# Causal attention and a gated feed-forward on one core: engine orders searched anew, with the 16-bit product sums kept apart from GpSimd's masks in the plan

## Chip, core and metric

The kernel runs on one core of a Trainium2 chip. The metric is device time in microseconds (us) of one launch; the time before is the median of three runs, 325.62 us. Engines are named as the profile names them: PE (TensorE; PEld its weight loads), DVE (VectorE), ACT (ScalarE), POOL (GpSimd) and SP (SyncE). POOL computes the masks and also issues most of the loads; SP issues stores and transposing transfers.

## What is computed

Inputs are float32. Attention has 8 batches, 8 heads, 576 tokens, 64 features a head, and 16 extra "beacon" keys that every query sees. Its result, 4608 tokens by 512 features, goes through a feed-forward of width 2048.

```python
k_all = np.concatenate([beacon_k, k], axis=2)
v_all = np.concatenate([beacon_v, v], axis=2)
scores = scale * np.matmul(q, k_all.transpose(0, 1, 3, 2))
causal[:, Nb:] = np.triu(np.ones((S, S), dtype=bool), k=1)
scores = np.where(causal, -1000000000.0, scores)
a = np.exp(scores - scores.max(-1, keepdims=True))
a /= a.sum(-1, keepdims=True) + 1e-09
x = np.matmul(a, v_all)                  # then tokens by heads*features
h = x @ w_in                             # 512 -> 2048
g = h * (1.0 / (1.0 + np.exp(-1.702 * h)))
out = g @ w_out                          # 2048 -> 512
```

## The kernel before

**Attention.** Work is cut into 16 sets (a batch and four of its heads; set s belongs to batch s // 2). For a set, PE makes scores in chunks (`e_qk`, L557 and L568, into the score banks `s`), ACT exponentiates a chunk into the fp16 tile `E` (`e_exp`, L580), and POOL sets the masked triangle of each key block to zero in place (`e_mask`, L598). From set 4 on, four DVE sums add the key blocks of `E` into `zs` (`e_zadd`, L616), so that PE's row-sum matmuls are short. A set then has four value tiles on PE (`e_av`, L656): first the row sums (name `av s.2.0`), which DVE transposes, inverts and spreads (`e_z1` L666, `e_z2` L672 and L677), then `av s.0.0`, `av s.0.1`, `av s.1.1`, each multiplied by the inverse on DVE and put into `xT` (`e_norm`, L694).

**Feed-forward.** Tokens go in groups: groups 0 and 1 of 256, groups 2 to 9 of 512. The first layer of a group is either plain (`e_m1`, L718) or, for part of the later groups, a seven-product Strassen form: products `f g.i.1` to `f g.i.7` (`e_part`, L923), with DVE sums of weights (`wsum`) and tokens (`xsum`) before them, ACT copies between them (`seedb`, `seede` L933, `keep7` L939) and DVE sums in PSUM after them (`sum22`, `sum21`, L942). ACT applies the gate (L740, L948). The second layer of groups 2 to 9 is a seven-product Strassen form too: `e_prod` (L836), named `m2.g.p.n0` for product p. DVE makes its inputs with the **product sums** `s g.i.n0` (16 of 128 x 512 fp16 a group, 128 in all, both inputs in SBUF) and its outputs with the joins (`e_join`, L852), which add a product in PSUM to `osb` and so free its PSUM bank. All two-input fp16 sums of DVE, product sums among them, go through `add`, L784.

**Banks.** Four PSUM banks are shared in turn by value tiles, first-layer tiles and products; four more serve the scores or, late, the Strassen tiles. `BANK` says which bank each tile takes. A tile that takes a bank waits for whatever reads the tile before it there.

**Order.** Nothing on the chip schedules. Each unit of work is an operation of a `Plan`, numbered in the order in which the kernel names them; `ORDER` gives for every engine the list of these numbers, found by a search outside the kernel, and `Plan.run` lays the lists out in time by fixed costs. The operations are emitted by planned start, and each engine then runs its own list strictly in turn; dependences become semaphore waits. In `Plan.run` an operation with `port` 1 (certain DVE sums) starts no earlier than the end of the last one with `port` 2 (POOL masks), and the other way round. That rule exists in the plan alone: nothing of it is emitted, and the chip runs two such instructions whenever their lists and semaphores let it.

Numbers used below: 362, 367 and 373 are group 2's joins of products 7, 5 and 4; 348, 349 and 350 its product sums `s2.2.*`; 375 is PE's `m2.2.3.0`; 488 a `wsum`, 490 to 493 group 3's `xsum`, 481 and 485 norms of set 5; 494 is `f3.0.1`; 626 is `qk27`. 1011 is `z2` of set 11 and 938 group 5's join of product 2; 993 and 1016 are `av10.1.1` and `av11.1.1`; 925 to 928, 934, 936, 914 to 920 are product sums of group 5. 1225 is `z2` of set 13, 1095 group 6's join of product 2, 1230, 1179 and 1177 are `av13.1.1`, `av12.1.1` and `av12.0.1`, 1103 is `m2.6.7.2`; 1082 to 1085, 1091 and 1094 are product sums of group 6. 402 and 403 are the transposes of set 4's keys and queries, 404 is `qk16`. 795 is the last mask of set 8, 800 the `zadd` that needs it, 801 `av8.2.0`, 845 a mask of set 9 that needs the exponentials 814 and 843.

Of the kernel before, what the change touches and what calls it, by code (L numbers as in the profile page):

```python
# [18 lines left out]
        126, 136, 162, 165, 231, 129, 168, 171, 236, 147, 150, 152, 131, 245, 238, 174, 177, 241, 192, 195, 262,  # L19
        201, 198, 204, 267, 248, 207, 210, 186, 269, 250, 252, 276, 187, 180, 272, 213, 188, 404, 181, 182, 183,  # L20
        189, 407, 257, 255, 283, 281, 288, 286, 279, 410, 222, 223, 224, 225, 417, 314, 296, 320, 300, 308, 298,
        312, 294, 310, 306, 324, 302, 316, 318, 334, 322, 304, 343, 216, 435, 426, 335, 217, 218, 219, 438, 336,
        344, 345, 337, 358, 353, 467, 359, 346, 354, 355, 356, 363, 364, 597, 429, 477, 360, 361, 433, 600, 431,
        482, 484, 480, 605, 365, 369, 366, 494, 370, 624, 371, 372, 375, 498, 376, 626, 496, 377, 503, 378, 502,
        516, 510, 500, 530, 512, 514, 526, 506, 518, 519, 538, 522, 532, 528, 540, 536, 534, 550, 559, 629, 615,
        551, 552, 560, 553, 569, 561, 570, 780, 574, 575, 571, 562, 572, 783, 576, 579, 577, 580, 638, 786, 618,
        622, 620, 643, 792, 641, 645, 581, 582, 585, 810, 651, 586, 587, 657, 588, 813, 591, 592, 593, 594, 655,
        653, 842, 659, 660, 663, 667, 697, 689, 693, 671, 669, 673, 685, 675, 676, 687, 695, 683, 679, 691, 707,
        801, 852, 968, 708, 716, 717, 718, 719, 709, 710, 804, 971, 859, 806, 857, 808, 855, 976, 742, 726, 727,
        743, 736, 728, 995, 731, 732, 737, 729, 733, 997, 738, 734, 739, 744, 745, 865, 1000, 748, 869, 749,  # L30
        750, 751, 871, 881, 887, 867, 873, 883, 874, 885, 905, 877, 889, 890, 907, 893, 903, 897, 921, 911, 899,
        901, 909, 922, 1009, 986, 1151, 923, 930, 931, 932, 940, 941, 924, 933, 1154, 993, 1016, 1012, 989, 942,
        1157, 945, 943, 1014, 991, 1163, 956, 946, 950, 951, 947, 1181, 948, 957, 1022, 952, 953, 1184, 958,
        959, 962, 1026, 963, 964, 965, 1213, 1031, 1024, 1030, 1062, 1028, 1038, 1064, 1044, 1068, 1034, 1042,
        1040, 1054, 1046, 1047, 1066, 1050, 1056, 1087, 1060, 1058, 1088, 1172, 1223, 1355, 1089, 1078, 1079,
        1080, 1090, 1081, 1102, 1103, 1358, 1230, 1179, 1177, 1228, 1175, 1363, 1104, 1107, 1097, 1098, 1226,
        1382, 1099, 1100, 1108, 1105, 1109, 1384, 1113, 1114, 1110, 1236, 1115, 1387, 1119, 1120, 1238, 1121,
        1116, 1240, 1242, 1252, 1258, 1122, 1245, 1244, 1254, 1268, 1373, 1256, 1248, 1284, 1270, 1260, 1261,
        1272, 1288, 1290, 1264, 1286, 1396, 1276, 1292, 1274, 1277, 1293, 1401, 1380, 1376, 1378, 1403, 1399,
        1280, 1308, 1296, 1317, 1409, 1309, 1425, 1318, 1319, 1411, 1310, 1427, 1311, 1429, 1320, 1327, 1431,  # L40
        1415, 1332, 1433, 1413, 1328, 1434, 1437, 1329, 1330, 1417, 1333, 1441, 1334, 1421, 1335, 1445, 1443,
        1337, 1447, 1457, 1418, 1338, 1339, 1459, 1449, 1463, 1340, 1461, 1453, 1450, 1481, 1465, 1343, 1344,
        1466, 1482, 1483, 1349, 1490, 1345, 1469, 1346, 1491, 1350, 1532, 1351, 1352, 1548, 1492, 1536, 1534,
        1493, 1484, 1505, 1550, 1552, 1506, 1516, 1507, 1517, 1556, 1554, 1500, 1501, 1557, 1502, 1503, 1518,
        1508, 1538, 1560, 1540, 1541, 1564, 1519, 1510, 1511, 1568, 1512, 1570, 1513, 1544, 1573, 1572, 1566,
        1522, 1580, 1523, 1524, 1525, 1584, 1576, 1586, 1582, 1588, 1589, 1604, 1605, 1613, 1606, 1592, 1614,
        1615, 1628, 1629, 1607, 1630, 1616, 1633, 1623, 1631, 1624, 1625, 1626, 1634, 1635, 1636, 1637, 1641,
        1642, 1643, 1647, 1644, 1648, 1651, 1652,
# [3 lines left out]
        237, 239, 175, 178, 242, 193, 196, 263, 199, 202, 205, 268, 208, 211, 270, 273, 405, 214, 190, 184, 408,  # L52
        411, 418, 419, 321, 226, 309, 299, 297, 301, 315, 295, 325, 317, 311, 307, 303, 313, 319, 323, 305, 436,
        220, 439, 468, 342, 469, 598, 601, 607, 606, 495, 625, 499, 627, 497, 511, 501, 531, 517, 515, 507, 509,
        505, 513, 539, 525, 533, 527, 529, 521, 541, 523, 537, 535, 630, 558, 781, 784, 787, 793, 794, 811, 658,
        652, 814, 656, 843, 844, 662, 668, 666, 654, 690, 698, 672, 674, 664, 686, 670, 678, 694, 688, 696, 682,
        684, 680, 692, 969, 715, 972, 977, 978, 996, 998, 866, 1001, 870, 882, 872, 868, 886, 884, 888, 880,
        906, 876, 878, 904, 908, 892, 894, 898, 896, 912, 900, 902, 910, 1152, 929, 1155, 1158, 1165, 1164,
        1182, 1023, 1185, 1027, 1214, 1215, 1025, 1029, 1065, 1039, 1033, 1063, 1045, 1043, 1035, 1055, 1037,
        1069, 1049, 1067, 1053, 1051, 1041, 1061, 1057, 1059, 1356, 1086, 1359, 1364, 1365, 1383, 1385, 1237,  # L60
        1388, 1239, 1241, 1253, 1243, 1259, 1255, 1251, 1269, 1257, 1247, 1249, 1285, 1271, 1263, 1273, 1267,
        1289, 1265, 1287, 1291, 1275, 1295, 1279, 1281, 1297, 1283, 1410, 1426, 1412, 1299, 1428, 1316, 1430,
        1432, 1436, 1414, 1438, 1416, 1442, 1440, 1420, 1422, 1444, 1446, 1458, 1448, 1424, 1460, 1462, 1452,
        1464, 1456, 1454, 1468, 1472, 1470, 1533, 1549, 1535, 1551, 1553, 1489, 1555, 1559, 1537, 1539, 1563,
        1565, 1561, 1543, 1569, 1571, 1545, 1547, 1575, 1581, 1579, 1585, 1567, 1583, 1587, 1577, 1591, 1593,
        1595, 1612, 1656,
# [3 lines left out]
        228, 127, 229, 259, 157, 164, 161, 167, 128, 130, 170, 173, 148, 149, 153, 151, 132, 246, 260, 176, 261,  # L70
        179, 194, 197, 247, 200, 203, 249, 206, 401, 209, 212, 403, 253, 254, 277, 251, 402, 278, 215, 258, 284,
        282, 256, 285, 416, 414, 280, 287, 415, 289, 422, 423, 424, 425, 486, 290, 291, 292, 326, 487, 329, 327,
        427, 331, 339, 333, 330, 338, 328, 428, 332, 293, 473, 340, 341, 474, 351, 357, 475, 476, 349, 347, 478,
        430, 479, 434, 432, 483, 485, 481, 490, 491, 362, 492, 350, 348, 367, 373, 493, 488, 489, 379, 504, 611,
        508, 520, 524, 612, 613, 542, 634, 614, 546, 545, 544, 554, 543, 547, 555, 548, 556, 616, 617, 549, 557,
        635, 563, 564, 567, 636, 637, 573, 578, 639, 640, 619, 565, 623, 621, 642, 644, 646, 647, 648, 583, 649,
        650, 589, 566, 595, 661, 797, 798, 665, 799, 848, 677, 699, 703, 681, 849, 800, 850, 851, 701, 700, 704,
        702, 802, 803, 711, 720, 853, 854, 712, 706, 805, 724, 705, 807, 713, 860, 856, 721, 809, 722, 858, 714,
        730, 861, 862, 863, 735, 740, 746, 723, 1005, 864, 752, 875, 1006, 879, 891, 913, 917, 1007, 895, 982,
        983, 984, 914, 985, 1008, 918, 925, 926, 915, 987, 919, 988, 1010, 1011, 934, 927, 936, 916, 938, 920,  # L80
        994, 935, 928, 990, 1013, 1017, 1018, 944, 1015, 1168, 937, 992, 1169, 949, 1019, 1020, 954, 1021, 960,
        1170, 966, 1219, 1220, 1032, 1036, 1048, 1052, 1073, 1221, 1070, 1171, 1071, 1075, 1077, 1222, 1072,
        1173, 1174, 1076, 1074, 1224, 1225, 1083, 1085, 1094, 1095, 1082, 1231, 1084, 1180, 1091, 1229, 1178,
        1176, 1369, 1370, 1227, 1232, 1093, 1101, 1233, 1371, 1106, 1234, 1235, 1092, 1111, 1392, 1117, 1372,
        1123, 1250, 1246, 1374, 1393, 1394, 1262, 1266, 1395, 1375, 1397, 1398, 1294, 1278, 1402, 1381, 1377,
        1282, 1379, 1400, 1300, 1304, 1301, 1312, 1298, 1302, 1405, 1406, 1407, 1306, 1305, 1313, 1408, 1321,
        1404, 1314, 1325, 1322, 1303, 1307, 1323, 1315, 1435, 1439, 1331, 1419, 1336, 1423, 1451, 1473, 1324,
        1474, 1455, 1341, 1467, 1478, 1475, 1479, 1471, 1487, 1347, 1528, 1529, 1477, 1353, 1476, 1496, 1485,
# [1458 lines left out]
```

## Time and profile before

| | us |
|---|---|
| median of 3 runs (325.38 to 325.70) | 325.62 |
| the profiled execution | 324.99 |
| its span, first to last instruction | 323.3 |
| busy: PE / PEld / DVE / ACT / POOL | 310.8 / 227.6 / 243.4 / 226.9 / 137.6 |
| granted TensorE clock, mean | 0.997 |
| share of 16 DMA engines: queue of POOL's loads / queue of the rest | 68.9% / 23.6% |

A profile row names an engine, a line of the kernel, the tiles written and read and a shape. A busy PE need not be PE at its peak, since matmuls are pipelined; so the waits, in which an engine stood idle for a named semaphore, are read beside the busy time. Rows of the timeline give start and length in us, "x4" merges neighbours of one kind, and brackets hold the idle time before a row and what ended it. Four PE matmuls of 256 columns start 0.44 us apart from the next four.

### The profile page before, as it was taken

Reading aid. Unit: us, or ns where it says so; the run is one execution under the profiler, and the core shown is the slowest. Engines: PE = TensorE matmul, PEld = TensorE weight load, DVE = VectorE, ACT = ScalarE, POOL = GpSimd, SP = SyncE. Lnnn points to the kernel's source line nnn. Section 1 sums busy time; section 2 is a strip of 40 time slices with the busy share of each in tenths; the row PEclk is TensorE's granted clock in tenths of the full one; section 3 lists DMA queues with packets and bytes.
Section 4 is the critical chain, followed back from the end, with each engine's and each line's share of the span. In section 5 each row is a group of like instructions: output and inputs, shape, how many; then the busy total and the mean of one; then the engine's idle time right before and its main releaser. Section 6 shows DMA issues by size and latency. Waiting matters only on the chain.

```text
span 323.3 us, 9042 instructions
## 1 busy us (share of the span) xinstructions
PE 310.8 (96%) x3835; PEld 227.6 (70%) x3835; DVE 243.4 (75%) x481; ACT 226.9 (70%) x297; POOL 137.6 (43%) x188
## 2 busy tenths in 40 slices
PE   6999999999997999999999989999999999999994
PEld 2567765545775667766788567766688888888883
DVE  4759893786989779768977798839977993775682
ACT  1778967567766896699668975798689658546720
POOL 8768658798469802175248105570132000000000
PEclk9999999999999999999999999999999999999998
DMA  6999999999999993559099933998006000020202
GB/s 116 175 203 193 173 197 159 162 118 132 204 110 141 205 153 62 76 141 131 2 92 98 149 100 49 179 134 78 2 3 146 4 32 3 0 99 32 100 33 99
DMA packets 125993, 34.67 MB, mean 107 GB/s; under 512 B 111488, under 2 KB 123904, under 8 KB 125952
## 3 DMA queue, kind: packets, MB, share of 16 engines
q0 software_dynamic: 91872, 18.57, 68.9%
q1 hardware_dynamic: 33872, 15.45, 23.6%
q8 instruction: 30, 0.49, 0.6%
q10 hardware_dynamic: 208, 0.07, 0.1%
q14 instruction: 11, 0.09, 0.1%
HBM read 37.22 MB, written 15.42 MB: 163 GB/s over the span
## 4 chain that ended last, share of the span: by engine, by line
PE 44%; DVE 10%; ACT 5%; issue 1%; DVEq 0%; ACTq 0%
PE u L836 21%; PE u L923 15%; PE u L656 4%; PE s L557 3%; DVE g L784 2%; PE u L718 2%; DVE zs L616 2%; DVE rz L677 2%; ACT g L948 1%; DVE sA L784 1%; ACT g L740 1%; DVE zt L666 1%; DVE u L942 1%; DVE osb L852 1%; ACT u L933 1%
## 5 line engine op out<-in xcount | busy, mean ns | idle before, releaser
L580 ACT ACTIVATE E<-s 128x2048 f16<-128x2048 f32 (+3 forms) x59 | 90.8, 1553 | 36.7 <-PE s L557 23.9
L598 POOL TENSOR_SCALAR_AFFINE_SELECT E<-E 128x512 f16<-128x512 f16 (+3 forms) x78 | 60.2, 850 | 103.7 <-ACT E L580 85.1
L836 PEld LDWEIGHTS <-g 128*128 128x128 f16 x768 | 73.1, 98 | 14.4 <-issue 3.2
L836 PE MATMUL u<-w,g 128*128 128x256 f16 x512 | 67.5, 273 | 1.7 <-DVE osb L852 1.7
L718 PE MATMUL u<-xT,w 128*128 128x512 f16 (+1 forms) x320 | 60.4, 337 | 0.0
L948 ACT ACTIVATE g<-u 128x512 f16<-128x512 f32 x80 | 46.6, 617 | 14.0 <-PE u L923 7.2
L852 DVE SCALAR_TENSOR_TENSOR osb<-u,osb 128x512 f32<-128x512 f32 (+2 forms) x51 | 33.2, 655 | 20.0 <-PE u L836 18.0
L718 PEld LDWEIGHTS <-w 128*128 128x128 f16 x320 | 30.5, 98 | 20.5 <-issue 0.3
L472 POOL DMA_DIRECT2D vb<-in_v_dram x32 | 40.1, 1259 | 0.6 <-issue 0.6
L923 PEld LDWEIGHTS <-SF 128*128 128x128 f16 x320 | 30.9, 98 | 8.0 <-issue 1.4
L836 PE MATMUL u<-tB,g 128*128 128x256 f16 x256 | 34.9, 273 | 0.0
L923 PE MATMUL u<-sig,SF 128*128 128x256 f16 x240 | 34.4, 273 | 0.1
L933 ACT ACTIVATE u<-u 128x512 f32<-128x512 f32 x40 | 23.6, 593 | 10.0 <-PE u L923 8.7
L656 PE MATMUL u<-E,vb 128*32 128x352 f16 (+8 forms) x928 | 28.1, 263 | 2.3 <-DVE osb L852 1.6
L740 ACT ACTIVATE g<-u 128x512 f16<-128x512 f32 x48 | 27.3, 637 | 4.0 <-PE u L718 3.8
L694 DVE TENSOR_TENSOR xT<-u,rz 128x352 f16<-128x352 f32 (+6 forms) x58 | 26.0, 478 | 5.3 <-PE u L656 4.8
L784 DVE TENSOR_TENSOR g<-g 128x512 f16<-128x512 f16 x64 | 28.3, 455 | 0.6
L656 PEld LDWEIGHTS <-vb 128*32 128x32 f16 (+1 forms) x928 | 20.3, 96 | 9.2 <-issue 4.8
L923 PEld LDWEIGHTS <-w 128*128 128x128 f16 x240 | 23.2, 98 | 3.4 <-issue 0.3
L616 DVE TENSOR_TENSOR zs<-zs,E 128x1344 f16<-128x1344 f16 (+2 forms) x36 | 22.1, 619 | 4.5 <-POOL E L598 3.4
L923 PE MATMUL u<-xT,w 128*128 128x256 f16 x160 | 23.7, 273 | 0.0
L486 POOL DMA_DIRECT2D qD<-in_q_dram x10 | 23.1, 2365 | 0.0
(72 smaller groups left out, 431.6 us busy)
## 6 DMA issues: line engine op xcount, KB each, us to landing
out_dram<-osb SPq DMA_DIRECT2D x35, 256.0 KB, 3.3
vb<-in_v_dram POOLq DMA_DIRECT2D x24, 128.0 KB, 7.2
qD<-in_q_dram POOLq DMA_DIRECT2D x10, 288.0 KB, 8.6
kD<-in_k_dram POOLq DMA_DIRECT2D x10, 288.0 KB, 9.8
w<-in_moe_w_in_dram POOLq DMA_DIRECT2D x8, 256.0 KB, 8.5
w<-in_moe_w_out_dram POOLq DMA_DIRECT2D x4, 512.0 KB, 10.9
kn<-in_k_dram POOLq DMA_DIRECT2D x6, 288.0 KB, 6.8
qn<-in_q_dram POOLq DMA_DIRECT2D x6, 288.0 KB, 6.9
```

What stands on the lines that cost most here:

```text
L472: nc.gpsimd.dma_start(out=t[0 : hi - lo, j, h0:h1, :], in_=v[b, h0:h1, lo:hi, :].rearrange("h n d -> n h d"),)
L580: nc.scalar.activation(out=Es[s][:, h0:h1, c0:c1], in_=sall[(i, p)][:, :, o : o + c1 - c0], func=AFT.Exp, scale=0.125,)
L598: nc.gpsimd.affine_select(out=blk, in_=blk, compare_op=ALU.is_ge, fill=0.0, base=off + (Nb if j == 0 else 0), pattern=[[0, Q], [1, w]], ch ...
L616: nc.vector.tensor_tensor(out=t, in0=E[:, :, Z0:S] if i == 1 else t, in1=E[:, :, wcol[i] : wcol[i] + S - a], op=ALU.add,)
L656: nc.tensor.matmul(u[32 * h : 32 * h + 32, a:e], lhs, src[0:kw, h, col : col + e - a], start=first, stop=last, skip_group_check=s >= EARLY ...
L718: nc.tensor.matmul(u[:, o + a - t0 : o + e - t0], w1t[:, kp, nt * P : (nt + 1) * P], xT[:, kp, a % XR : (e - 1) % XR + 1], start=(kp == 0 ...
L740: nc.scalar.activation(out=gts[g][:, n0:n1, 0:w], in_=rings[("m1", g, n0)][:, 0 : n * w].rearrange("p (n w) -> p n w", n=n), func=AFT.Gelu ...
L784: (nc.vector if eng == "DVE" else nc.gpsimd).tensor_tensor(out=out, in0=a, in1=b, op=op)
L836: nc.tensor.matmul(u[:, HM * mt : HM * (mt + 1)], lhs[:, n, mt * P : (mt + 1) * P], rhs[:, n, :], start=(n == 0 and (mt == 0 or apart) and ...
L852: nc.vector.scalar_tensor_tensor(out=osbs[(g, dst)][:, c0:c1], in0=rings[("p", g, p)][:, c0:c1], scalar=scale_of(g), in1=osbs[(g, src)][:, ...
L923: nc.tensor.matmul(u[:, HM * n : HM * (n + 1)], lhs[x][:, (2 * i + n) * P : (2 * i + n + 1) * P], rhs[:, x, :], start=fresh and n == 0 and ...
L948: nc.scalar.activation(out=gts[g][:, n : n + 2, HM * h : HM * (h + 1)], in_=rings[src][:, :].rearrange("p (n w) -> p n w", n=2), func=AFT. ...
```

## The change

`Plan.op` strips digits and dots, no longer digits alone, from the end of an operation's name before it looks it up in `HELD`. Names of product sums (`s2.0.4`) so end as `s`, which is in `HELD`; before, they ended as `s2.0.`, which is not. `zadd`, `xsum`, `wsum`, `t`, DVE's own masks and `bk` had matched already. With that rule `ORDER` and `BANK` were searched anew. The set of operations, their dependences and what each emits are the same (3826 matmuls in both programs); the positions differ: 184 of PE's 578 list entries stand where they stood, 101 of DVE's 437, 135 of ACT's 288 and 40 of POOL's 181, with mean moves of 2.6, 2.9, 1.6 and 7.6 places. The count of PE's changes between its three tilings is 128 in both.

```diff
-        elif eng == "DVE" and name.rstrip("0123456789") in HELD:
+        elif eng == "DVE" and name.rstrip("0123456789.") in HELD:
             o.port = 1
```

Of `ORDER`, the places that the prediction speaks of:

```diff
     "PE": [
-        201, 198, 204, 267, 248, 207, 210, 186, 269, 250, 252, 276, 187, 180, 272, 213, 188, 404, 181, 182, 183,
+        201, 198, 204, 267, 248, 207, 210, 186, 269, 252, 250, 276, 187, 180, 272, 181, 182, 213, 404, 188, 183,
...
-        482, 484, 480, 605, 365, 369, 366, 494, 370, 624, 371, 372, 375, 498, 376, 626, 496, 377, 503, 378, 502,
+        482, 484, 480, 605, 365, 366, 369, 370, 494, 624, 371, 372, 375, 498, 376, 626, 377, 503, 378, 496, 502,
...
-        901, 909, 922, 1009, 986, 1151, 923, 930, 931, 932, 940, 941, 924, 933, 1154, 993, 1016, 1012, 989, 942,
+        909, 921, 986, 1009, 1151, 930, 922, 923, 931, 932, 933, 924, 940, 1154, 941, 1016, 993, 1012, 989,
...
-        1080, 1090, 1081, 1102, 1103, 1358, 1230, 1179, 1177, 1228, 1175, 1363, 1104, 1107, 1097, 1098, 1226,
+        1088, 1089, 1090, 1081, 1102, 1358, 1230, 1179, 1228, 1177, 1175, 1363, 1097, 1098, 1107, 1099, 1226,
     "DVE": [
-        179, 194, 197, 247, 200, 203, 249, 206, 401, 209, 212, 403, 253, 254, 277, 251, 402, 278, 215, 258, 284,
+        176, 179, 247, 197, 194, 200, 206, 249, 203, 414, 209, 212, 253, 254, 277, 251, 402, 278, 403, 215, 256,
...
-        430, 479, 434, 432, 483, 485, 481, 490, 491, 362, 492, 350, 348, 367, 373, 493, 488, 489, 379, 504, 611,
+        478, 479, 434, 432, 483, 488, 481, 485, 362, 490, 367, 349, 491, 492, 493, 373, 350, 489, 611, 379, 612,
...
-        983, 984, 914, 985, 1008, 918, 925, 926, 915, 987, 919, 988, 1010, 1011, 934, 927, 936, 916, 938, 920,
+        984, 917, 985, 1008, 914, 918, 987, 915, 919, 988, 1010, 925, 927, 916, 936, 926, 1011, 938, 1017, 920,
...
-        1173, 1174, 1076, 1074, 1224, 1225, 1083, 1085, 1094, 1095, 1082, 1231, 1084, 1180, 1091, 1229, 1178,
+        1173, 1072, 1076, 1174, 1224, 1225, 1084, 1095, 1091, 1075, 1231, 1180, 1083, 1092, 1229, 1176, 1178,
     "POOL": [
-        826, 1125, 633, 631, 632, 785, 812, 788, 796, 822, 815, 846, 845, 782, 789, 828, 838, 766, 768, 1197,
+        632, 818, 633, 768, 772, 1125, 785, 1133, 1195, 788, 1191, 812, 845, 832, 776, 789, 815, 782, 1193, 770,
...
-        795, 1131, 973, 1133, 834, 847, 980, 1187, 970, 999, 830, 832, 1003, 1143, 1002, 836, 1004, 1135, 981,
+        796, 846, 1129, 836, 795, 970, 830, 999, 1141, 834, 980, 1003, 981, 1189, 1004, 979, 838, 828, 847, 973,
```

164 rows, old and new, of tables (BANK, ORDER) are left out of this document.

## The prediction

> **What bounds the kernel now.** Read first were the page's busy times and slices, then the view of who waited for whom.
>
> ```profile
> PE 310.8 (96%) x3835; PEld 227.6 (70%) x3835; DVE 243.4 (75%) x481; ACT 226.9 (70%) x297; POOL 137.6 (43%) x188
> ...
> PE   6999999999997999999999989999999999999994
> ...
> DVE  4759893786989779768977798839977993775682
> ```
>
> PE sets the time: it is busy in nearly every slice, and both programs have the same matmuls and as many changes of tiling. An order can win only what PE waits. Those waits (waiter, waited for: total us, times, longest) are:
>
> ```profile
> PE u L836 <- DVE osb L852: 1.7, 1, 1.7
> PE u L656 <- DVE osb L852: 1.6, 2, 1.0
> ...
> PE u L923 <- DVE u L942: 0.7, 2, 0.4
> PE u L656 <- DVE xT L694: 0.6, 2, 0.3
> ```
>
> That is 4.6 us in seven places, all for DVE: the ceiling of the gain, since other engines' waits matter only where PE ends up in one of its own.
>
> **What a clash costs.** The view of line 784 (times in ns, min/median/max) and the view by lines (busy us, mean ns) of the product sums:
>
> ```profile
> L784 DVE TENSOR_TENSOR g<-g x64: 381/418/1276, 79.2 to 312.4; 128x512 f16<-128x512 f16 x64
> ...
> L784 DVE TENSOR_TENSOR g<-sA,g x32: 382/420/1339, 79.7 to 311.4; 128x512 f16<-128x512 f16 x32
> ```
> ```profile
> L784 DVE TENSOR_TENSOR g<-g 128x512 f16<-128x512 f16 x64 | 28.3, 455 | 0.6
> ...
> L784 DVE TENSOR_TENSOR g<-sA,g 128x512 f16<-128x512 f16 x32 | 15.4, 488 | 0.8
> ```
>
> A product sum takes 0.42, and up to 1.34. The excess of the means over the medians is 64 x 37 + 32 x 68 ns = 4.5 us. This is DVE time; it counts only where a join or a norm queued behind it lets PE go. So I go to PE's waits one by one and ask what each becomes in the new lists.
>
> **Stall A, at 99 us.** Timelines (start, length) of DVE, POOL, PE and ACT:
>
> ```profile
> 93.23 1.09 DVE L694 TENSOR_TENSOR xT<-u,rz 128x352 f16<-128x352 f32 x2 [0.46 <-PE u L656]
> 94.63 1.06 DVE L694 TENSOR_TENSOR xT<-u,rz 128x352 f16<-128x352 f32 x2 [0.30 <-PE u L656]
> ...
> 96.08 0.96 DVE L784 TENSOR_TENSOR sig<-xT,sig 128x512 f16<-128x512 f16 x1
> 96.97 0.68 DVE L852 SCALAR_TENSOR_TENSOR osb<-u,osb 128x512 f32<-128x512 f32 x1
> 97.57 0.80 DVE L784 TENSOR_TENSOR sig<-xT,sig 128x512 f16<-128x512 f16 x1
> 98.29 2.01 DVE L784 TENSOR_TENSOR g<-g 128x512 f16<-128x512 f16 x2
> 100.22 1.48 DVE L852 SCALAR_TENSOR_TENSOR osb<-u,osb 128x512 f32<-128x512 f32 x2
> ```
> ```profile
> 97.72 2.13 POOL L472 DMA_DIRECT2D vb<-in_v_dram  x1
> 98.62 3.26 POOL L598 TENSOR_SCALAR_AFFINE_SELECT E<-E 128x512 f16<-128x512 f16 x3
> ```
> ```profile
> 98.17 1.05 PE L836 MATMUL u<-tB,g 128*128 128x256 f16 x8
> 100.95 0.60 PE L836 MATMUL u<-w,g 128*128 128x256 f16 x4 [1.74 <-DVE osb L852]
> ```
> ```profile
> 98.28 1.88 ACT L580 ACTIVATE E<-s 128x2048 f16<-128x2048 f32 x1
> ```
>
> Product sums 350 and 348 stand before join 367 and, against three masks, take 2.01 instead of twice 0.42; the join starts at 100.22 and `m2.2.3.0` waits 1.74. In the new lists both stand elsewhere. After the second norm (ends 94.3) come `wsum` 488 (as much data as three to four product sums, 1.3), two norms and join 362 (0.6 each), `xsum` 490 (0.4), then 367. The 0.30 in which DVE waited is filled; the norms end near 96.6, 362 near 97.2, 490 near 97.6, and 367 at 98.25, before PE asks at 99.0. The wait goes: -1.74. But the norms end some 0.9 later than they did (94.63 + 1.06 = 95.7), and `f3.0.1`, which needs them, stands 0.44 later in PE's list. So its copy on ACT, and the exponential queued behind it (98.28, ends 100.16), end 0.45 later, at 100.6, and `qk27` waits for its score bank where PE comes at 100.3. I take 0.45 back: **-1.3**. Bounds: -1.74; and -0.5, if 490 and 488 suffer as the rows of 0.96 and 0.80 did (the second while POOL only issued a load).
>
> [...]
>
> **Stall B, at 193 us.** DVE, then PE:
>
> ```profile
> 190.60 0.38 DVE L784 TENSOR_TENSOR g<-g 128x512 f16<-128x512 f16 x1
> 190.91 0.80 DVE L784 TENSOR_TENSOR g<-sA,g 128x512 f16<-128x512 f16 x1
> ...
> 192.49 0.68 DVE L852 SCALAR_TENSOR_TENSOR osb<-u,osb 128x512 f32<-128x512 f32 x1
> ```
> ```profile
> 191.51 0.75 PE L656 MATMUL u<-E,vb 128*32 128x352 f16 x20
> 193.22 1.33 PE L656 MATMUL u<-E,vb 128*32 128x352 f16 x52 [0.96 <-DVE osb L852]
> ```
>
> Four product sums, one of 0.80, stand between inverse 1011, which ends at 190.6, and join 938, which frees the bank of `av11.1.1`. After, three of them stand ahead of 1011 and 938 follows it directly: 1011 ends some 1.0 later, at 191.6 (three sums, 0.34 from one start to the next), 938 at 192.3. `BANK` gives `av11.1.1`, now first, a bank that product 1 held: it needs only 1011 and waits 0.2 beyond 191.5. `av10.1.1` takes 938's bank and waits 0.15. 0.96 becomes 0.35: **-0.6** (0 to -0.96).
>
> **Stall C, at 228 us.** DVE, then PE:
>
> ```profile
> 225.49 1.16 DVE L784 TENSOR_TENSOR g<-sA,g 128x512 f16<-128x512 f16 x2
> ...
> 227.03 0.68 DVE L852 SCALAR_TENSOR_TENSOR osb<-u,osb 128x512 f32<-128x512 f32 x1
> ```
> ```profile
> 227.76 2.19 PE L656 MATMUL u<-E,vb 128*32 128x352 f16 x76 [0.65 <-DVE osb L852]
> ```
>
> Three product sums between 225.49 and join 1095 become one, and `av12.1.1` takes product 1's bank instead of the join's. The 0.65 goes; but `m2.6.7.2` (0.44), which filled PE while `qk50` had its exponential pending, now comes later, and some 0.25 of it is lost: **-0.4** (-0.65 to +0.2). The smaller of the two waits on L942 (0.24, `f8.1.3` at 266 us) ends too, since five other pieces of PE, not three, now stand between `f8.1.5`, which its sum needs, and `f8.1.3`: **-0.2** (0 to -0.24). The other waits keep their neighbours: 0.
>
> **New waits.** Query transpose 403 moves behind key transpose 402 and inverse 278. DVE, then PE:
>
> ```profile
> 47.50 1.26 DVE L523 STREAM_TRANSPOSE kT<-kn 128x576 f32<-128x576 f32 x1
> ...
> 48.82 0.48 DVE L677 STREAM_TRANSPOSE rz<-rc 128x288 f32<-128x288 f32 x1
> ```
> ```profile
> 49.51 0.63 PE L568 MATMUL s<-qT,kT 32*128 32x512 f16 x8
> 50.07 3.63 PE L764 MATMUL u<-w,g 128*128 128x512 f16 x16
> ```
>
> 278 ends at 49.3 now, and 0 to 1.1 earlier with 403 gone from ahead of it; 403 (1.26, as 402) then ends between 49.5 and 50.6. `qk16`, which needs it, comes one PE piece later (four such take 3.63), at 50.4: **+0.2** (0 to 0.5). Near 85 us two product sums move ahead of set 5's `zadd`, in a stretch where the slices show DVE 8 or 9 tenths busy, and `av5.2.0` waits for that `zadd`: **+0.1** (0 to 0.7, both sums). A walk finds old waits more surely than new ones; for those not found I add **+0.3**, an estimate: one more wait of the size of the smaller ones above (0 to 3, the sizes of A, B and `qk16` together).
>
> POOL's loads move most (sets 8 to 15). I cost that at nothing: what hides it are the tens of us between those loads and their sets' first use. The price where that cover is thin is rival 1.
>
> Sum: -1.3 - 0.6 - 0.4 - 0.2 + 0.2 + 0.1 + 0.3 = **-1.9**. The profiled execution's own 324.99 (span 323.3 and 1.7 around it) becomes 323.1. It was 0.63 below the median, so the median goes from 325.62 to **323.7**.
>
> **Rivals.**
>
> 1. *Masks late behind loads (slower).* All of set 8's late masks now stand behind mask 845, which waits for the later of two exponentials, and six masks and six issues, 845 among them, come before mask 795, which `zadd` 800 and then `av8.2.0` need. The exponentials, PE, and POOL's busy time (count) per stretch, fifth pair of numbers, and one issue's length in the crowded stretch from 60 to 140 us:
>
> ```profile
> 139.99 1.94 ACT L580 ACTIVATE E<-s 128x1024 f16<-128x1024 f32 x2
> ```
> ```profile
> 152.47 0.38 PE L656 MATMUL u<-zs,ones 128*32 128x288 f16 x8
> ```
> ```profile
> 60.00:80.00 20.00, 20.00 (x144) 9.65 (x143) 13.56 (x20) 13.63 (x22) 19.54 (x21) 1.00 1.86 127
> ...
> 140.00:160.00 20.00, 19.30 (x224) 12.90 (x227) 17.23 (x32) 18.33 (x26) 8.97 (x12) 1.00 0.73 111
> ```
> ```profile
> L472 POOL DMA_DIRECT2D vb<-in_v_dram x10 | 19.9, 2000 | 0.0
> ```
>
> 845 starts at 141.0. At 8.97 / 12 = 0.75 an instruction, 795 as the thirteenth ends at 150.8, in time for 152.5. At 19.54 / 21 = 0.93 it ends at 153.1, and from there each 0.1 costs PE 1.3. At 1.15, between that and the 2.0 of a single issue, it ends at 156.0 and PE stands 3.5: 325.6 + 3.5 - 1.9 = 327.2. Against it: POOL has 0.75 in that very stretch. Chance 0.24.
>
> 2. *No change.* A clash is waited out by one side anyway, and the plan only chooses whom. Sums gone from 99 us stand before set 5's `zadd` and behind join 367, and PE waits there: A -0.5, B and C 0, new waits +0.5. Median 325.6. For it: DVE is as busy on either side of A. Against: B's and C's tiles get other banks. Chance 0.18. [...]
>
> 3. *All waits go.* Then -4.6 + 0.6 = -4.0: 321.6. Against it: value tiles still take joins' banks. Chance 0.12.
>
> 4. *It does not do what it says.* Lists that keep sums and masks apart in planned time still let them meet on the chip, as the `xsum` at 96.08, held already, met one. The excess of 4.5 stays and only the moved joins help, -1.0: 324.6. It is part of the forecast's range and chance.
>
> **How the numbers follow.** Forecast, with 4: chance 0.46, own range 322.6 to 324.8. Up to 0.2% (0.65 us) a measurement of this kernel cannot tell from no change. Faster 0.46 + 0.12 = 0.58, same 0.18, slower 0.24. The range, 322.3 to 327.0, runs from the inner side of rival 3 to just short of rival 1.
>
> **What would show it.** Right: no idle of 1.74 before L836 near 97 to 101, product sums' means under 0.44, mask 795 done by 151, PE's waits for DVE near 2.5 in total. Wrong: PE waiting over 1 us on `zs` near 90 or from 150 to 157, or over 0.5 at `qk16`; waits for DVE still above 4; any PE wait for a load.

## The result and the profile after

| | before | after |
|---|---|---|
| median, four runs each | 325.50 us | 328.72 us (327.84 to 329.46) |
| ratio, 95% interval | | 1.0101 (1.0072 to 1.0131) |
| the profiled execution / its span | 324.99 / 323.3 | 328.67 / 327.0 |
| granted TensorE clock, mean | 0.997 | 0.986 |

The change made the kernel 1% slower; the forecast was 323.7 us. The page after, busy times and four rows of the slices:

```profile
PE 313.0 (96%) x3835; PEld 228.9 (70%) x3835; DVE 242.9 (74%) x481; ACT 227.1 (69%) x297; POOL 138.3 (42%) x188
...
PE   6999999999999999869999999999999999999994
...
DVE  4759884948989489736884988587988875766863
...
PEclk9999999999999999959999999999999999999998
```

The hole in PE that stood in slice 13 (99 us) is gone. A new one stands in slices 17 and 18 (131 to 147 us), and the granted clock, which was 9 throughout, falls to 5 in slice 18. The view of who waited for whom names it (waiter, waited for: total us, times, longest):

```profile
PE s L557 <- DMA qT<-qD: 3.9, 1, 3.9
...
PE u L836 <- DVE xT L694: 0.6, 1, 0.6
PE u L923 <- DVE u L942: 0.5, 1, 0.5
PE u L656 <- DVE xT L694: 0.4, 2, 0.3
PE u L656 <- DVE zt L666: 0.3, 1, 0.3
...
PE u L923 <- DVE osb L852: 0.3, 1, 0.3
```

PE's waits for DVE fell from 4.6 us to 2.1 us. (Both lists also hold 2.6 us at L1510 at the very start and 0.3 for ACT; the prediction's 4.6 and this 2.1 leave them out, and they are the same in both.) One wait for a transfer, of a kind that before did not have, is larger than all that was won.

**What was late.** From set 6 on, queries and keys come in two steps: POOL issues a load into a staging buffer in memory (`st`, L486), and SP issues a transposing transfer from there (`xbar`, L490) into `qT` and `kT`. Set 10's transposes are 840 (keys) and 841 (queries); `qk35` needs both. The timeline after, POOL and SP's queue, then PE:

```profile
125.88 3.23 POOL L486 DMA_DIRECT2D kD<-in_k_dram  x2
128.06 1.70 POOL L598 TENSOR_SCALAR_AFFINE_SELECT E<-E 128x512 f16<-128x512 f16 x1
128.64 2.67 POOL L486 DMA_DIRECT2D qD<-in_q_dram  x1
129.09 2.24 SPq L490 DMA_TRANSPOSE kT<-kD  x1
131.42 3.68 SPq L490 DMA_TRANSPOSE qT<-qD  x1
```
```profile
136.96 0.60 PE L923 MATMUL u<-xT,w 128*128 128x256 f16 x4
141.43 1.03 PE L557 MATMUL s<-qT,kT 64*128 64x256 f16 x12 [3.87 <-DMA qT<-qD]
142.40 1.04 PE L923 MATMUL u<-sig,SF 128*128 128x256 f16 x4
```

Three loads (1133 and 1195, keys of sets 13 and 15; 1191, queries of set 14) go out just ahead of the two transposes. In the profile before they go out at 160, 202 and 102 us, and POOL issued no load from 112 to 137 us. The view of line 490 says what happened to the transposes, first before (130 to 136 us), then after (128 to 136 us), us from issue to landing, of two transposes each:

```profile
DMA to landing us min/median/max: 4.3/4.4/4.5
```
```profile
DMA to landing us min/median/max: 9.8/9.8/9.9
```

The 841 that was issued at 131.42 landed at 141.3, and PE, 1.9 us ahead of before, had stood since 137.6.

**What followed it.** The stretches after, as in the prediction (fifth pair POOL, then the granted clock):

```profile
137.00:140.00 3.00, 0.56 (x6) 0.26 (x3) 1.55 (x2) 0.99 (x2) 0.00 (x0) 1.00 1.84 150
140.00:143.00 3.00, 1.57 (x15) 1.24 (x16) 0.00 (x0) 0.50 (x1) 0.00 (x0) 0.52 0.70 198
143.00:146.00 3.00, 2.99 (x16) 1.94 (x14) 2.38 (x3) 2.97 (x4) 2.35 (x4) 0.50 0.68 124
146.00:149.00 3.00, 3.00 (x15) 1.47 (x14) 1.79 (x3) 1.83 (x4) 3.00 (x5) 0.84 1.47 179
```

From 140.2 to 147.0 the granted clock was half: four matmuls of 256 columns took 1.04 at 142.40 that take 0.60 at 136.96. PE counts as busy there, which is why its busy time rose by 2.2 us although the matmuls are the same.

**Where the 3.4 us at PE's end came from**: starts of PE pieces in the two profiles, at places where both lists have run the same pieces. From start to start a wait reads 0.1 to 0.2 us longer than in the list of waits, which counts from the modelled end of the piece before it.

| next piece | before | after | shift | what lies between |
|---|---|---|---|---|
| `m1.0.14` | 33.79 | 34.11 | +0.3 | a wait of 0.3 for `zt` |
| `m2.2.3.0` | 100.95 | 99.23 | -1.7 | stall A gone: -2.0 |
| `f3.0.3` | 109.19 | 107.72 | -1.5 | a wait of 0.3 for a join |
| `f4.0.2` | 138.81 | 136.96 | -1.9 | |
| `qk35` | 139.34 | 141.43 | +2.1 | the transfer: +3.9 |
| `m1.4.6` | 151.08 | 155.12 | +4.0 | the clock: +2.0 |
| `m2.5.1.2` / `av10.2.0` | 185.62 | 190.57 | +5.0 | `f5.0.3`'s wait behind `zadd` 1005, about +0.7; the rest not followed |
| `av11.0.0` | 193.79 | 197.55 | +3.8 | stall B gone: -1.2 |
| `m2.6.5.2` | 234.12 | 237.86 | +3.7 | stall C, 0 |
| end of PE | 318.74 | 322.14 | +3.4 | |

### The profile page after: what moved, and what is told of

The parts are those of the page before. It is cut to its first block, busy times and chain, and to the rows that moved or that the text cites. A ratio compares the mean times of both kernels' runs of the same rounds, so it can differ in the third digit from the quotient of the medians.

```text
span 327.0 us, 9039 instructions
## 1 busy us (share of the span) xinstructions
PE 313.0 (96%) x3835; PEld 228.9 (70%) x3835; DVE 242.9 (74%) x481; ACT 227.1 (69%) x297; POOL 138.3 (42%) x188
## 4 chain that ended last, share of the span: by engine, by line
PE 44%; DVE 6%; ACT 6%; DMA 3%; issue 1%; SPq 0%; DVEq 0%; ACTq 0%
PE u L836 20%; PE u L923 15%; PE u L656 4%; PE u L718 3%; DMA qT<-qD 3%; PE s L557 2%; ACT g L740 2%; ACT g L948 2%; DVE g L784 2%; DVE rz L677 1%; DVE osb L852 1%; DVE xT L694 1%; ACT u L933 1%; DVE zt L666 1%; ACT E L580 1%
## 5 line engine op out<-in xcount | busy, mean ns | idle before, releaser
L598 POOL TENSOR_SCALAR_AFFINE_SELECT E<-E 128x512 f16<-128x512 f16 (+2 forms) x78 | 58.5, 827 | 86.9 <-ACT E L580 74.7
L948 ACT ACTIVATE g<-u 128x512 f16<-128x512 f32 x80 | 45.5, 608 | 16.0 <-DVE u L942 8.5
L718 PEld LDWEIGHTS <-w 128*128 128x128 f16 x320 | 30.8, 98 | 22.0 <-issue 1.1
L836 PE MATMUL u<-tB,g 128*128 128x256 f16 x256 | 35.6, 273 | 0.6 <-DVE xT L694 0.6
L472 POOL DMA_DIRECT2D vb<-in_v_dram x32 | 31.3, 1000 | 3.1 <-PE u L656 3.1
L740 ACT ACTIVATE g<-u 128x512 f16<-128x512 f32 x48 | 26.8, 615 | 4.1 <-PE u L718 3.9
L616 DVE TENSOR_TENSOR zs<-zs,E 128x1344 f16<-128x1344 f16 (+2 forms) x36 | 24.2, 680 | 3.8 <-POOL E L598 3.2
L923 PEld LDWEIGHTS <-w 128*128 128x128 f16 x240 | 23.6, 99 | 4.1
L557 PE MATMUL s<-qT,kT 64*128 64x80 f16 (+22 forms) x320 | 20.5, 255 | 3.9 <-DMA qT<-qD 3.9
```

The lines of the kernel that those rows point to most:

```text
L472: nc.gpsimd.dma_start(out=t[0 : hi - lo, j, h0:h1, :], in_=v[b, h0:h1, lo:hi, :].rearrange("h n d -> n h d"),)
L598: nc.gpsimd.affine_select(out=blk, in_=blk, compare_op=ALU.is_ge, fill=0.0, base=off + (Nb if j == 0 else 0), pattern=[[0, Q], [1, w]], ch ...
L718: nc.tensor.matmul(u[:, o + a - t0 : o + e - t0], w1t[:, kp, nt * P : (nt + 1) * P], xT[:, kp, a % XR : (e - 1) % XR + 1], start=(kp == 0 ...
L740: nc.scalar.activation(out=gts[g][:, n0:n1, 0:w], in_=rings[("m1", g, n0)][:, 0 : n * w].rearrange("p (n w) -> p n w", n=n), func=AFT.Gelu ...
L836: nc.tensor.matmul(u[:, HM * mt : HM * (mt + 1)], lhs[:, n, mt * P : (mt + 1) * P], rhs[:, n, :], start=(n == 0 and (mt == 0 or apart) and ...
L923: nc.tensor.matmul(u[:, HM * n : HM * (n + 1)], lhs[x][:, (2 * i + n) * P : (2 * i + n + 1) * P], rhs[:, x, :], start=fresh and n == 0 and ...
```

## The experiments

Theory: the three loads occupy the transfer engines when set 10's transposes need them; the wait and the half clock behind it cost some 6 us, and without them the new order is faster than the old. Rival explanations: the transposes are slow of themselves; the wait only moves on; the low clock costs nothing. Each ratio is to the kernel before, run on the same chip beside it (324.9 us there).

| run | median us | ratio, 95% interval |
|---|---|---|
| 1: three loads behind mask 846 | 328.12 | 1.0093 (1.0075 to 1.0112) |
| 2: load 1191 alone behind 846 | 324.57 | 0.9996 (0.9982 to 1.0009) |
| 3: before, with the three loads early | 326.94 | 1.0069 (1.0047 to 1.0092) |
| 4: after, idle matmuls in the wait | 327.14 | 1.0065 (1.0051 to 1.0078) |
| 5: three loads behind mask 795 | 323.48 | 0.9948 (0.9931 to 0.9965) |
| 6: after again | 328.42 | 1.0097 (1.0081 to 1.0113) |
| 7: before, joins ahead of 350, 348 | 326.72 | 1.0040 (1.0022 to 1.0057) |
| 8: run 5 and `zadd` 1005 later | 322.98 | 0.9925 (0.9911 to 0.9940) |
| 9: before, 348 early, 350 late | 326.12 | 1.0029 (1.0005 to 1.0053) |
| 10: three loads behind mask 812 | 323.43 | 0.9951 (0.9935 to 0.9966) |
| 11: run 10 and `zadd` 1005 later | 323.10 | 0.9941 (0.9919 to 0.9963) |
| 12: run 7 again, one execution | 327.12 | |

**Run 1.** `ORDER["POOL"]` of after (the loads' planned transfers in `Q` move along, here and in the other runs that move loads):

```diff
-        632, 818, 633, 768, 772, 1125, 785, 1133, 1195, 788, 1191, 812, 845, ...
-        796, 846, 1129, 836, 795, ...
+        632, 818, 633, 768, 772, 1125, 785, 788, 812, 845, ...
+        796, 846, 1133, 1195, 1191, 1129, 836, 795, ...
```

> The changed kernel with loads 1133, 1195 and 1191 taken from ahead of the transposes of set 10 (840, 841) to behind mask 846 on POOL, some 20 us later; nothing else moves. Theory (the loads fill the transfer engines ahead of the transposes): 840 and 841 land 4 to 5.5 us after issue instead of 9.8 and 9.9, PE's wait of 3.9 us at qk35 is gone, the granted clock stays 1.00 from 141 to 147, and the time is 328.7 - 3.9 - 2.2 = 322.6 us (322 to 323.5). Rival (the transposes are slow of themselves, or SP issues them late): they still take over 9 us and the time stays at 328 to 329. Second rival (the wait only moves): the transposes of set 11, or masks behind the moved loads, wait instead, 325 to 327.

The transposes landed in 4.3 and 4.7 us and `qk35` did not wait, as the theory has it, and yet the time stayed: the second rival. POOL and PE:

```profile
145.84 3.21 POOL L486 DMA_DIRECT2D kD<-in_k_dram  x2
...
148.02 4.26 POOL L486 DMA_DIRECT2D qD<-in_q_dram  x2
...
150.17 3.03 POOL L472 DMA_DIRECT2D vb<-in_v_dram  x1
...
151.09 2.61 POOL L598 TENSOR_SCALAR_AFFINE_SELECT E<-E 128x320 f16<-128x320 f16 x1
...
154.11 0.38 PE L656 MATMUL u<-zs,ones 128*32 128x288 f16 x8 [2.99 <-DVE zs L616]
```

Put ahead of mask 795, the loads made it end at 153.70, and `av8.2.0` waited 3.0 us for its `zadd`; the clock fell behind this wait too (slice 20, from 155 us, shows 7). It is the place and the mechanism of the prediction's first rival, brought about by the edit.

**Run 2.** The same, with 1191 alone moved.

> The changed kernel with load 1191 alone taken to behind mask 846; 1133 and 1195 stay ahead of the transposes. Theory, by bytes in the queue: 1195 landed at 137.5 with 1191 sharing the engines and should land near 134 without it; 841 lands by 137.5, so PE waits 0 to 0.5 us at qk35 and the time is 322.6 to 323.5 us. Rival (any load issued just ahead of a transpose makes it slow): 841 still takes over 8 us, PE waits over 2 us, 326 us or more.

The view of line 490 (128 to 136 us):

```profile
DMA to landing us min/median/max: 7.1/7.7/8.2
```

841 took 4.3 us with none of the loads (run 1), 7.1 with 1195 still under way, 9.9 with 1195 and 1191: 2.8 us for each load of 288 KB (1133 landed at 131.4, as 841 was issued). The figure is that of 841: with both loads it took 9.9 again in run 6 and 9.1 in run 4, and 840, issued two us earlier, went from 4.7 to 8.2 and 9.8 in less even steps. The wait at `qk35` was 0.8, beyond the forecast's 0.5. The time missed the forecast by a us: 1191, at its new place, made mask 795 end at 151.7, and 0.75 us of wait followed at 154 us. Run 5, without either wait, is 1.1 us faster.

**Run 3.** Before, `ORDER["POOL"]` (the loads are taken out of their old places further on):

```diff
-        826, 1125, 633, 631, 632, 785, 812, ...
+        826, 1125, 633, 631, 632, 785, 1133, 1195, 1191, 812, ...
```

> The kernel before with the three loads put behind mask 785, just ahead of its transposes of set 10, and nothing else changed. Theory: 840 and 841 land near 141 to 142 instead of 135.5 and 136.6, PE waits 2 to 3 us at qk35, the clock falls for some us behind it: 325.5 + 2.5 + 2 = 330 us (327.5 to 331). Rival (the wait needs the rest of the new order): 325.5 us.

The transposes took 9.4 and 8.8 us and landed at 141.6 and 139.4; PE waited 2.7 us at `qk35`, in an order that is otherwise that of before. The clock held (1.00 from 137 to 146 in the profile), so the loss is 2.0 us and not the 4.5 of the forecast. The loads alone are enough for the wait.

**Run 4.** In `e_qk`, after the score tile is taken:

```diff
+            if i == 35:
+                for _ in range(18):
+                    nc.tensor.matmul(sc[:, 0, :], w1t[:, 0, 0:P], w1t[:, 0, 0:512], start=True, stop=True)
```

> The changed kernel with 18 idle matmuls of 512 columns (18 x 0.216 = 3.9 us) on PE ahead of qk35's own, into the score tile that qk35 overwrites; the transposes still land late. Theory (the idle time and the lower clock behind it are two prices): the clock stays 1.00 from 141 to 147 and the matmuls there are 0.109 us apart, so the time falls by the clock's share alone, 328.7 - 2.2 = 326.5 us. Rival (the late landing is the whole price, the low clock runs beside waits that are there anyway): 328.7 us.

The clock stayed at 1.00 and pieces behind `qk35` took 0.60. The time fell by 1.0 us against run 6 (1.0065 to 1.0097), not by 2.2: the idle matmuls end at 142.5, 1.1 us after `qk35` could start in the profile after and 2.0 after 841 landed in this one (131.4 and 9.1 us), so part of what the clock gave back was lost to them. All six executions kept a mean clock of 0.997 or more.

**Run 5.** The three loads, taken from their places as in run 1, behind mask 795.

```diff
-        796, 846, 1129, 836, 795, 970, ...
+        796, 846, 1129, 836, 795, 1133, 1195, 1191, 970, ...
```

> The changed kernel with the three loads behind mask 795 on POOL. With them ahead of it, as in the first of these runs, the transposes landed 4.7 and 4.3 us after issue and qk35 did not wait, but mask 795 ended at 153.7 and PE waited 3.0 us for its zadd 800. Theory (two waits of one kind, each from loads put where something else is due): with both out of the way neither wait is left, PE's waits are those of the run with one load moved less 0.8 and 0.75, and the time is 0.993 to 0.996 of before, 322.6 to 323.6 us where before is at 324.9. Rival (the loads delay something wherever they go; next the transposes of sets 12 and 13 or mask 970): PE waits over 1 us on a DMA or on zs again, 325 or more.

Neither wait is left: 841 landed at 135.1, mask 795 ended at 149.1, `av8.2.0` started at 151.2. The time is 0.5% below before, as forecast. One wait is new: near 205 us `qk48`, which needs the key transpose of set 14, stood 0.7 us (0.9 in run 8, 1.1 in run 10). That transpose landed 7.2 to 7.7 us after its issue in these three, just as PE started; it took 5.6 in after and at most 6.2 in run 11, where PE did not wait. Why it was slower is open.

**Run 6.** After, unchanged.

> The changed kernel once more, beside the others on one chip. Theory: 3 to 4.5 us of wait at qk35 every time, since its transposes stand behind two loads, and 1.007 to 1.013 of before. The granted clock behind the wait decides the rest: where a profile shows 1.00 from 141 to 147 the execution should be some 2 us shorter than where it shows 0.50. Rival (the wait comes and goes with the chip): 324 to 325 us in some rounds.

The wait was there again, 3.5 us in the profile. That execution kept its clock (0.998) and took 326.33 us; the four others, at 0.986 to 0.994, took 327.60 to 328.94. The same kernel:

```profile
140.00:143.00 3.00, 1.75 (x22) 1.45 (x23) 0.90 (x2) 1.52 (x2) 0.42 (x1) 1.00 0.56 160
143.00:146.00 3.00, 2.97 (x20) 1.81 (x19) 1.15 (x2) 2.97 (x5) 2.94 (x5) 1.00 1.02 188
```

Against the 328.67 of the first profile that is 2.3 us less. PE's starts were 0.2 us ahead before the wait and 0.4 more came from the shorter wait, so the half clock costs some 1.7 us (2.0 in the table of starts, against before).

**Run 7.** Before, `ORDER["DVE"]`: stall A alone.

```diff
-        ... 491, 362, 492, 350, 348, 367, 373, 493, ...
+        ... 491, 362, 492, 367, 373, 350, 348, 493, ...
```

> The kernel before with product sums 350 and 348 behind joins 367 and 373 on VectorE, nothing else. Theory (stall A came from those two sums alone, which met masks): the wait of 1.74 us near 99 us is gone, m2.2.3.0 starts near 99.2, and no new wait of over 0.4 us takes its place: 1.3 to 1.7 us less than before, ratio 0.995 to 0.996. Rival (the clash is waited out wherever the sums stand): the wait returns within 10 us and the ratio is 1.000.

`m2.2.3.0` did start at 99.3. But the two sums met the masks behind the joins as well, and `m2.2.3.2` needs 348:

```profile
100.09 2.23 DVE L784 TENSOR_TENSOR g<-g 128x512 f16<-128x512 f16 x2
...
102.38 0.61 PE L836 MATMUL u<-w,g 128*128 128x256 f16 x4 [2.06 <-DVE g L784]
```

**Run 9.** Before, with 348 where the change puts it, ahead of `zadd` 473, and 350 behind the joins.

```diff
-        427, 331, 339, 333, 330, 338, 328, 428, 332, 293, 473, ...
-        ... 362, 492, 350, 348, 367, 373, 493, ...
+        427, 331, 339, 333, 330, 338, 328, 428, 332, 293, 348, 473, ...
+        ... 362, 492, 367, 373, 350, 493, ...
```

> The kernel before with two product sums moved: 348 to ahead of zadd 473 (84 us, where the changed kernel has it), 350 to behind joins 367 and 373. The run before this one in kind left 348 behind the joins, and PE waited 2.1 us for that sum itself at m2.2.3.2. Theory (stall A is worth what the changed kernel gained there, and 348 is what has to move far): no wait over 0.4 us between 97 and 105 us, 1.7 to 2.0 us less than before, ratio 0.994 to 0.995. Rival (moving it is paid at zadd 473 or av5.2.0 near 90 us): ratio 0.998 to 1.000.

The stall at 99 us and that of run 7 at 102 us are gone; the clash went to the `wsum` behind them, 5 us later, and the clock fell there too (0.50 from 108 to 110 us):

```profile
105.90 0.28 PE L923 MATMUL u<-sig,SF 128*128 128x256 f16 x1 [1.84 <-DVE SF L784]
```

So neither move of the two sums had the gain at A. After, `wsum` 488 and 348 both stand earlier and 367 ahead of 350; that all of it is needed is likely, but no run moved just these. Six of the twelve executions took 324.5 to 325.7 us, six 326.5 to 327.7; in the latter the mean clock was 0.995 or below, in the others 0.997 or above.

**Run 12.** Run 7 again, for the clock.

> The kernel before with product sums 350 and 348 behind joins 367 and 373 once more, for its profile: its twelve executions fell into two groups, four of 324.9 to 325.5 us at a mean granted clock of 1.000 and eight of 326.4 to 327.4 at 0.994 or 0.995. Theory: the second group has a stretch of some 3 to 4 us at half clock, and it lies right behind the wait of 2.1 us at 100.3 us. Rival: the low clock lies elsewhere (at the end, behind the last matmul, where the kernel before has 0.95) and costs nothing; the group's time has another cause.

The wait was the same (2.07). The same stretches in run 7, at 325.50 us, and in run 12, at 327.12 us:

```profile
102.00:105.00 3.00, 2.62 (x26) 2.00 (x27) 3.00 (x6) 1.42 (x1) 3.00 (x6) 1.00 2.01 194
105.00:108.00 3.00, 3.00 (x25) 2.25 (x23) 1.20 (x2) 2.97 (x5) 3.00 (x6) 1.00 1.64 238
```
```profile
102.00:105.00 3.00, 2.44 (x17) 1.46 (x18) 3.00 (x5) 0.88 (x1) 3.00 (x7) 0.70 2.01 194
105.00:108.00 3.00, 3.00 (x22) 2.37 (x21) 1.49 (x3) 2.88 (x3) 3.00 (x6) 0.73 1.64 238
```

The theory's place and length hold. The difference is 1.6 us; PE's starts were already 0.2 apart before the stretch, so the price of the clock by itself is some 1.4 us.

**Runs 8 and 11.** `zadd` 1005 behind the sums, on run 5 and on run 10.

```diff
-        722, 714, 723, 863, 864, 730, 735, 740, 752, 746, 1005, 875, 895, 891, 879, 1006, ...
+        722, 714, 723, 863, 864, 730, 735, 740, 752, 746, 875, 895, 891, 879, 1005, 1006, ...
```

> The run with the three loads behind 795, and zadd 1005 on VectorE put behind the four sums 875, 895, 891 and 879. There it took 3.21 us beside masks 1004 and 979 and two load issues (1.12 in the kernel before), and f5.0.3 waited 0.7 us near 182 for sum 875 behind it. Theory: zadd takes under 2 us at its new place, that wait is gone, 0.5 to 0.7 us less than without this edit, ratio about 0.992. Rival (it meets the next masks, 847, 973 and 1002, and is as long there, and av11.2.0 waits instead): no gain.

The `zadd` in after, while POOL went through three masks and three load issues (two of the masks are shown), and in run 8 four places later:

```profile
178.36 1.55 POOL L598 TENSOR_SCALAR_AFFINE_SELECT E<-E 128x320 f16<-128x320 f16 x2
178.39 3.21 DVE L616 TENSOR_TENSOR zs<-E 128x1856 f16<-128x1856 f16 x1
```
```profile
177.35 1.12 DVE L616 TENSOR_TENSOR zs<-E 128x1856 f16<-128x1856 f16 x1
```

It took 1.12 there, and of the two waits on L942 one went from the list. 0.9925 is the fastest measured, 0.75% below before, though its interval and that of run 5 still touch. On run 10 the same edit gave less:

> The run with the loads behind mask 812, and zadd 1005 behind sums 875, 895, 891 and 879 as in the best run so far (ratio 0.9925). Theory: the two edits add up, ratio 0.992 to 0.993, 322.3 to 322.8 us. Rival: over 0.994.

0.9941 against 0.9951, a difference inside both intervals; the forecast of 0.992 to 0.993 was missed. That the edit is worth 0.3 to 0.7 us is likely and not shown.

**Run 10.** The loads one mask later than in after: behind 812, at 135 to 139 us.

```diff
-        ... 1125, 785, 1133, 1195, 788, 1191, 812, 845, ...
+        ... 1125, 785, 788, 812, 1133, 1195, 1191, 845, ...
```

> The changed kernel with the three loads one mask later: from around mask 788 to behind mask 812, that is from 126 to 129 us to some 135 to 139 us, where the transposes of set 10 have been issued. Theory (what is queued first lands first): 840 and 841 land under 5 us after issue, qk35 waits nothing, the transposes of set 11 (needed at 161) take the delay of 6 us and more in their place and hide it; time as with the loads behind 795, ratio 0.994 to 0.996. Rival (transfers share the engines fairly, whatever came first, or the loads delay mask 795 again): PE waits over 1 us at qk35 or av8.2.0, ratio over 1.000.

Set 10's transposes took 4.7 and 5.2 us. Set 11's, issued at 138.0 and 139.9, inherited the delay (line 490, 137 to 145 us):

```profile
DMA to landing us min/median/max: 7.4/8.6/9.9
```

Nobody waited for them at their own use; the gain is that of run 5. Loads at 126 us cost 5 us, and the same loads 9 us later cost nothing. The runs don't tell a queue served in order from engines that share their time: here the first load went out at 134.99, when 841 landed.

## Why the prediction was wrong

The forecast was 323.7 us, in a range of 322.3 to 327.0; 328.72 came. The step that failed: "POOL's loads move most (sets 8 to 15). I cost that at nothing: what hides it are the tens of us between those loads and their sets' first use." The moved loads were indeed hidden. I asked of them when their own data are due, and not whose transfers they would go beside. At the new place two of them cost set 10's query transpose 2 x 2.8 us; its slack was 2.7 us before (841 landed at 136.6 and `qk35` came at 139.3), and PE had come 1.9 us nearer. 5.6 + 1.9 - 2.7 = 4.8, less what SP issued earlier (0.9): 3.9, and 3.9 came. The half clock behind the wait, some 2 us more, is a second price that the prediction has no term for. That the loads would stand there could be read from the new lists beforehand; the price of a load is known from run 2.

The kernel's planner has the same gap, so nothing in the plan spoke against this order. In `Plan.lat`, a transpose lands a fixed time after its issue, whatever the loads' lanes hold, so the plan starts `qk35` at the same 135.8 us in both programs:

```python
        if d.name[:4] == "xbar":
            return 5000 if o.eng != "SP" else 0
```

The other terms, against the profiles:

- *A, forecast -1.3.* Measured -2.0. The score wait that I took back for `f3.0.1` did not come, and `xsum` 490 ran at 0.42 (at 97.19) while POOL issued a load (from 97.25), and not at the 0.80 of the prediction's row. In runs 7 and 9, with `wsum` 488 left behind the joins, the clash returned within 5 us; that 488 is the piece that matters fits this and was not tested alone.
- *B, -0.6.* -1.2: the whole wait, 0.96 in the list and some 0.2 more from start to start.
- *C, -0.4.* 0. The 0.65 went, and PE lost 0.2 near 231 us and waited 0.60 at 233.65, for norms behind product sums.
- *266 us, -0.2.* -0.3.
- *`qk16`, +0.2, and 90 us, +0.1.* Neither wait is in the list.
- *Not found, +0.3.* 0.3 near 32 us, 0.3 at 104, 0.7 near 182: 1.3.
- *The sum, -1.9.* With the loads put elsewhere, runs 5 and 10 show -1.5 by their medians. The sum was right to half a us, in part by luck: its terms that came out better were off by 1.7 us together, those that came out worse by 1.4, and runs 5 and 10 lose 0.7 and 1.1 us at 205 us, where after does not wait. The term outside the sum was not right.

Of the signs named beforehand: no idle of 1.74 near 97 to 101 us (right); PE's waits for DVE 2.1, forecast 2.5 (right); product sums' means under 0.44 (0.450 and 0.425, so half right); mask 795 done by 151 us (153.65, but only because `qk35` was late, see rival 1); "any PE wait for a load" was among the signs of error, and it came, at the transpose that the loads delayed.

*Rival 1* had the side, and loads of POOL as the cause, but looked for it on POOL itself. What it feared of the new list did not happen: in run 5, where POOL's list from 845 to 795 is that of after, 845 started at 139.6 and 795 ended at 149.1, 0.73 us an instruction against the 0.75 of the prediction, and PE did not wait. After, 795 ended at 153.65 because the exponential that 845 needs stood behind the late `qk35` (845 started at 143.6), and PE, late too, came for it at 156.8. The wait came in full only in run 1, with three loads more ahead of 795 (run 2, with one, had 0.75 us behind it).

*Rival 4* was partly right. Sums that the plan had always held apart took up the clashes that the product sums shed. The view by lines after (before had 22.1 and 15.0 here, 28.3 and 15.4 for the product sums):

```profile
L784 DVE TENSOR_TENSOR g<-g 128x512 f16<-128x512 f16 x64 | 27.8, 450 | 1.4 <-PE u L836 0.9
L616 DVE TENSOR_TENSOR zs<-zs,E 128x1344 f16<-128x1344 f16 (+2 forms) x36 | 24.2, 680 | 3.8 <-POOL E L598 3.2
L616 DVE TENSOR_TENSOR zs<-E 128x1856 f16<-128x1856 f16 x12 | 17.4, 1455 | 0.6 <-POOL E L598 0.6
...
L784 DVE TENSOR_TENSOR g<-sA,g 128x512 f16<-128x512 f16 x32 | 13.3, 425 | 3.2 <-PE u L836 2.8
```

Product sums lost 0.5 + 2.1 us of DVE time, the `zadd` gained 2.1 + 2.4, of which 1005 alone 2.1. Whether the rule gave the gain of run 5, or a fresh search without the rule would have found it too, no run shows.

## What to carry to other kernels

Cost a moved load twice: when its data are due, and which transfers with little slack (2.7 us here) are in flight where it now goes. A fixed latency in a plan (5 us here) misleads when it depends on what else is on the transfer engines: these transposes took 4.3 to 9.9 us, and each load of 288 KB in the way cost one of them 2.8 us. A PE wait of 2 to 4 us can cost another 1.4 to 2.0 us of half clock behind it, so one long wait can be worse than several short ones of the same sum: the seven waits before, 4.6 us in all and 1.74 at most, left the clock at 1.00.

## What the runs showed of the hardware

The half clock came in whole pieces. In run 12 the finer stretches put it from 103.2 to 106.6 us, 3.4 us, beginning 0.6 us after PE had started again; in run 9 from 107.7 to 111.1, again 3.4; in the profile after from 140.2 to 147.0, twice that, beginning 2.6 us into the wait:

```profile
102.50:103.00 0.50, 0.44 (x4) 0.31 (x4) 0.50 (x2) 0.00 (x0) 0.50 (x3) 1.00 1.67 216
103.00:103.50 0.50, 0.50 (x6) 0.25 (x6) 0.50 (x2) 0.00 (x0) 0.50 (x3) 0.70 1.52 263
...
106.00:106.50 0.50, 0.50 (x4) 0.37 (x3) 0.00 (x0) 0.48 (x2) 0.50 (x4) 0.50 1.37 270
106.50:107.00 0.50, 0.50 (x6) 0.41 (x4) 0.00 (x0) 0.50 (x1) 0.50 (x5) 0.89 1.35 273
```

The length of a wait alone does not tell whether the clock falls: a wait of 2.07 us lowered it in run 12 and one as long left it up in run 7, and one of 3.5 us left it up in run 6. Where a wait lies does better, as far as these profiles go. In the traces' record of the clock, every change in all fourteen profiles lies a whole multiple of 3.413 us behind the first rise: in the profile after 133.12, 139.95 and 317.44 us behind it (39, 41 and 93 times), before 314.03 (92 times). Counted in steps of that length from there, PE had stood idle 2.58 us (after), 2.07 (run 12), 1.93 (run 9) and 1.90 (run 1) in the step just ahead of each drop within the kernel, and 1.92 (run 6) or less in every step that no drop followed. Run 7's wait fell into two steps as 1.53 and 0.53, run 6's as 1.56 and 1.92, run 12's into one. So in these profiles the drop goes with the idle time inside one step, from some 1.9 us on (an estimate from these figures: the two sides overlap by 0.02 us, and the ends of matmuls are modelled). No run placed a wait at a chosen point of a step, so this is read from the profiles and not tested.
